# Layer norm with attention and a SwiGLU gate: the prologue's work is shared out anew among ScalarE, POOL and SP

## The chip, the cores and the metric

One core of one Trainium2 chip. The metric is the device time of one execution in microseconds; lower is better. The kernel before takes 1733.33 us (median of three runs, 1733.18 to 1734.9).

## The reference

```python
xn = layernorm(x)                       # x: 2048 tokens x 512, eps 1e-5
q, k, v = split(xn @ wqkv)              # 32 heads of 16
p = softmax(q @ k.T * 16**-0.5)         # full attention, 2048 x 2048 for each head
s = (p @ v) @ wo
h = silu(xn @ w1) * (xn @ w3)           # 1792 wide
return x + s * silu(h @ w2)
```

All in float32. A product of two float32 matrices is made of three matmuls on rounded parts: each operand is split into a high part (rounded) and a low part (the rest), and low x high, high x low and high x high are summed.

## The kernel before, in words

The 2048 tokens are 16 tiles of 128 (`t`) and four blocks of 512 (`b`).

**The prologue** (lines 449 to 668) normalises and transposes the tokens, makes the values of all heads, and the Q and K rows of the first eight heads. Its steps:
- `load_x(t)` fetches one token tile (nine buffers). Tiles 0 to 3 are fetched at the start; others as the work goes on.
- `spread(t)` makes mean and variance on VectorE (DVE), and the power -1/2 on POOL; `norm(t)` calls it, and normalises on DVE.
- `transposed(t)` turns a tile by four TensorE (PE) transposes; ScalarE (ACT) copies the high part, DVE makes the low part. Blocks 0 and 2 use one pair of buffers (`even_pair`), blocks 1 and 3 another.
- `token_rows(b, c)` multiplies a block with the K (`c` = 1) or Q (`c` = 0) weights: 12 matmuls; the high part by ACT, the low part by DVE; stored by ACT's and SP's queue. `load_k` and `load_q` fetch these rows back, arranged by head, in six copies each.
- `token_values(b, i)` multiplies one tile with the V weights: 12 matmuls, copies on ACT, a store from ACT's queue.
- `keep_tokens(b)` stores a block's transposed high and low part (1 MB each).
- `beside(b, n)` puts maxima of the first head pair between these steps, as many as `groups` says. One maximum (`max_unit`) is a matmul of 128 queries with 512 keys and a DVE reduction.
- `blank` lists arrays that POOL clears, among them `qs` and `ks[1]`, which `load_q` and `load_k` fill.

**The main stage.** There are 32 phases (16 head pairs, two halves of the queries). For each, the maxima of the scores are found first (`m`), they are appended to the queries as two more rows (`max_rows`, whose four copies to `qs` are line 446), and then come scores with their exponential on ACT (`s`) and the multiplication with the values (`v`). The gate's SwiGLU products (`f`) and the projection of the remaining Q and K rows (`rows_here`) run between them. Matmuls of `s`, `m` and `f` have at most 64 rows, so the upper and the lower half of the array work at the same time (small and capital letters). `ORDER_OF_ISSUE`, a text of some 9200 letters, says in which order the halves are issued; `r` and `R` place the row step, `o` the output's products. A letter whose work isn't ready by the kernel's own clock model is put off and issued later. PE takes its instructions in this order.

The gate's weights are fetched into four buffers, split by POOL and kept in a ring of nine places, the first four of which lie in `even_pair`; SP issues these loads in order with all its other copies. When the gate's last half is done, its memory is given back, and the loads for the output's products begin.

Seven PSUM banks are shared by all these products; the eighth (`pv`) holds the attention's sums.

Of the kernel before, what the change touches and what calls it, by code (L numbers as in the profile page):

```python
# [51 lines left out]
    "MfMfMffMMffMMffMffMffRfMffMfMffMmFfFFmFffFfFFfFFfFmFmFfffMffMffMfSFfFfsFFfFsfFFsmFFsFmFFffmFsFFmFsfF"  # L52
    "mFSfFsfMsFfFmSfFmFfSFfMfSffSsMvvvSmmFFsFsFffMsFFfmSfSfFmFsfFMsFFfmFMfSffMfSfmMvvMsSffMfFfSFmfSfFMsfF"
    "SmFfSfFmFsFFmsFFfmFMffMmMvvvSmsMFfFfFsfMFsfFmSfFsFmFsFfMsfFmFFfSfMffMfSMmvvSmSffMFfSfFmfSfFMsfFsFMff"
    "SFmSFfmFsFfFsFmMFfMmvvRsSMsFsvmSsFFmFfSfFfSmFfmSfFfSfFmFfSmFsFfMfFfMSfMmvvsMSsMmvFmsFFmFsFmFsFffSfMf"
    "SFfmSfFFmsFFffMMffMMsvvSfSsSmfMvvmSmSfFFfsFfMFsFfmSfFFsmFFsfMsFFfmFMfSffMfSfmMvvmSfSMfFfSfFmSffFMsFf"
    "FsMsFFfmsFFfMsFfmFFMfMfMmvvvMsfMSffSfFFmfSFmFsfFmFSfmFFsfFFmSffFFfMsfMMsvvRSmsFFmFsFffMfSFfFsmFsFfMs"
    "FfFmSfmFFfMffMsMvvsMfMfSfSfMfSffMsFfFmFsFFmfSfFsFmFfSFfSmfFfSmFFffMSffmFSfFmFfSmfFSfFsfFMsFfmFsFfFMf"
    "FsmFMmvvvsSFmmFMmvvvMsSffMfSfFFmfSFfMsFfSfMfSfFmFsFfMsFFfFffMSffMSfffMsFsFfFmFsFFmsFFfFmSfmFFsfMfFmM"
    "vvsMmSmSvvvsMmFFsfFFsfMsFfFmSfFsFmFSffMsfFmFFffSMffMfSMsvvRmSFsFfFmFsFfSmFsfFMffSfFMsfFFmSfmFFfSffMM"  # L60
    "mvvMfSfMfSffMfSfSffFMfSFfmSFffMsfFSfMfFsFmFsFmFsFFfmFfSfMMmvvmSmSmMvvMfSffMSfMffSfMfsFFsfFFmFsFfsMfF"
    "FsmFFsFfsMfFFmfSFfFssMfFfFmSfFsFmFFfMffSMfMfMfvvSssSsSvvvMssFFmsFmFFmFsFfFsfFFmSfFfSmFsfFMfSfFmfSFfM"
    "sFfSfMfSfFmFsFfMsFfMfSfMfFfSfMfMmvvMmMsMmvvvsMmFSfFfFsfMFsFfmSfFfSmFSfFfSmfFFsMfFsFfmFsFfMSfFfmFsFmF"
    "FsfFmFfMfSfSfSrvsSmSMmvvMffSMmmMvvFmFsFmsFmFFsFfFsfMsFfMfSfFsFmfFSfMsfFFmFsFmfFSffSFmFFsfMFfffMSfMff"
    "SfFFsmFFsFmFsfFmFSfFmSfmFfFFfMmmMvvvvSmfMfSFffSFmfSFmFsFmFfSfMFfsFfFsMSfFfmFFffMfSffMSfSffMFsFfmFsFm"
    "FsFFfmFsFFmfSfFFmmMvvsMmMMsvvmSSmMfrvmSfMfSSffFFmfSFmFsFmFfSfMfFsFfFsMSfFfmFFffMfSfMfSfSffMFsfFmFsFm"
# [12 lines left out]
    "fMfSffMSfMffSfFsFmFsFfFmSfFFmsFsFFfmFmFmMvvvMssSMmvfMSfMfSfMffSFfFsmFsFfMfSfmFFsFmFfSmfFFsmFFfMmvvvS"
    "mfMfSSfFfFmSfFfMsfFsFMsfFFmFsFfMsFfmFFMffSmMvvmSfFsMfFfSFmSffFSmFfSfMsFfFmSfFfMsFfFsFmFfSmSvvvvRMsMf"  # L80
    "fSFffSFfMsFffSMsFFfmSFffMsFMffFsFFmsFFffMsFFfmFsFfMsFfmFFsFFmfSfMFfsMFfFfMffMmMvvvMsfSfMfSfFFmFsFmFs"
    "fFFmSffFSmFfSfMfSfFmFfFfMfSfMfSfSffMfFsFmsFfFMsfFmFFsFFmsFFmfFmMvvvvMfSffMSffMfSfSfFmFsfFMsfFFmSFfFm"
    "sFfsFMFfsFmFffMSffMFfsFFmfSsFFfmFsFfMsFFfmSfFmfFFfmMMmvvvvmSSmfSfFfFFmfSfFSmFfSfFmfSFfmSfFFmFsFfFssM"
    "vvvvRfSMfSffMSffMFfsFmFfSsFFfmFsFfFmSfFFmsFfFfMMmvvMsfFsMFsFffMFsfMfSfMfFsFmfFSffFSmFsFfMsfFfMFffSMf"
    "SffSsSvvsSSsSsvvvMsSmmSvMffSMfSffMfSffSfMsFFfmSfFmFsFsFfFmFsFfMFsfFmFsFmFfSFsfFmFFsfFmSFffMfFMffMMfM"
    "fmMvvvvmSMsfFfFsFFmSfFmFsFfmFSfFmFsfFFsMfFsFmSFffMsFfmFSFfSfmSFffMSffFmSfMfMfMfFfsMvvvvRMsmFFssFFmFs"
    "FsFffFmFFsFmFsFFfmSffSFmSffFMfSfFmSfFMffSfMFfsMfFfSMfFfffMMfmMvvvvmSSfmFfFFsFmFsFmFsfFmFSfmFFssFFfMs"
    "fFFmsFFFmsfFmFFffSMfSMfffSfMfSfMfSfsFFfmFsFFmsFFfmFSfFmFsmFFfMffMmMvvvvSmSmFssFvvsMmFsFFfFsfMSffMfSf"
    "MfFsFmFfSfFfSmFfFfMfSfMfSffMsFsFFfFmFsFmsFfFFmSfFmFsfFfMfSfMmMvvMsSmmMvvmSMfFsfFFsfMsFFfmSfSfFmFsFfF"
    "mFfSfMfSfFmFfMmrvvSmSfFmsFfFfMsFFfmSfFsFmFFsFfmSFfmSfFffMfSfMMmvvvMsfSfMfSfFFmfSfFMsFfsFMfSfFmSffFMs"  # L90
    "FfsFFsFFffMfSffMFFfmFsFsfFMsFFfmFsFfMsFfFmFSfSfmMvvSsmSmMvvFmsFmFFsmFFsFffSfMSffMSffFMfsFMffSfSfFmFF"
    "ffMSffMfSfFmFsFFsfMFsFfmFsFFmsFFfmFMfMfmMvvvmSSmMmvvfMSffMSfMffSfFsFfMsFfFsFmFmFfSfsFFmSfFfFmFmrvMsf"
    "SMffFfSFmSfFfMsFfSmFfSfFmFsFFmsFFfmFMffMmSvvvvsMMffSFffSFmSfFmFsFmFfSfMfFsFSffMsFFfmfFFfMfSffMSffSfM"
    "sFfFmFsFmFsFFfmFsFFmsFfFMfMfSsSvvvvvmFsFmFFsFmFsFfSffMfSfMfSFfMfsFfMfSFfSfmFFffMSffMfsFFmFsFfFsMFfsF"
    "mFsFfMsFFfmFfMMffmMvvvmSSfMfFfsFfMfSfMfSfMfFsFmFfSfFsFmFsFfMsFfFmFfSfMfSffMsMvvmSSmSmvvvRfSMffSMffSf"
    "MfSfsFFmFFsfMfSfFmSfFFmfSffMFsSfFfMFsfFmsFFfMfSfFmsFmFFfSmfFFsFfFmMmvvvfMfSfMFsFfmFFsFmFsSffFMfFsfFS"
    "mFfsFMfsFFfMsFfFmSffFSfMsFfFmFsfFMfSffFMmfMvvvSmsMMmvvmFsFFmsFFmFsfFfSfMfSfMfSfFfMsFfMfSfSfFmSfFfMsF"
    "fFmFsFmFsFfFsFmSFfFfSfffMSsMvvvvvFmFsFmsFmFsFsFFmFmFsFffSfFMsfFmFSfFSfmSffFMSfFfmSFfmsFmFfFMmvvvMssM"
    "fFsFfFFfSmFfSmFfSfFmSfFfMfFsFmFsFfMfSfMrvmSmSsFFffFfMsFfFmSfFFsmFsFfMsFfmFSfFfMffSfMMmvvMsfSFmFfFsfM"
    "sFFfmSfFsFmFsFfMfSFfmSfFmFfSfMfSmvvvvFmsFmFFsFsFmFfSffMfSfMSfFffMsFfMfSfSfFmFFffMfSffMsFFmFsFFfsMFfs"  # L100
    "FmFsfFMsFfmFFMfffMMsvvsMSffMfSfFFmfSFfMsFfSmFSffFmFsFmFsFFfmFfSfMSmvvSmSsFmfFFffMFsfFmSfFsFmFsFfMsFf"
    "mFFffSMfMffSsMvvvvvRSmfSMffFSffFMsfFSfMfFsFmSffFMsFMffFsFFmsFFffMfSfFmFsFmFsFFfmFsFmFfSfMFfsFfMSfFff"
    "MmMvvsSSsmMvvvSmfMfSFfSfFmsFFmFsFmFfSfMFfsSfFfMSfFfmFfFfMfSfMfSffSfMsFfFmFsFmFsFFfmFsFFmFfFfMmMmvvMs"
    "MfmSMvvvMssFMsFfFfFmSfFfSmFfsFMfFsFfMsFfMfSffFFfMfSfMfSffMfSfsFFmFsfFMFsfFmSfFFmsfFfSFsFFsMmvvSmSssS"
    "vvvRSmFsfFFmFsFfmSfSfFmFsFfMsFfFmSfFmFfSfMffSfMSmvvvvSmsFmFfFFsfMFsFfmSfFSfmFfSFfmSFffMfSFffMFfMffSM"
    "ffSfFsFfMsfFFmFsFmFfSfmFFsmFFfFfMmmMvvvvMsfFfMsFFfMffSFmfSfFfSmFsFfFMsFfMfmFFfmFmMvvSmfSfMFfsFFmsFFf"
    "MsFfsFMfsFFfMsFfMfSffFFfMfSffMfSfMfSFfFsmsFFfMFsfFmsFFmFsFmFFfSffMmSvvvvSmfMfSfSfFFmfSfFMsFfsFMfFsfF"
    "MsfFMfSfsFFfmFFsSmvvvSmSfMfSffSfMmrvsMMffSfSfMfSffMfSfMfFsFmFfSfFFsmFFsfMfSfFmFsFmFsFfSfFmFFsfMSfFfm"
    "FsFFmsFfFfMSffMsSvvvvvFmFsmFsFFsmFsFmFFffSFmSFffMsfFfMSfSfFmfSfFMfSFfmSfFfMfSfMFfsFFmsFFffMMffMmMvvv"
    "SmSfMffSFfFmfSFfMsFfFsMfFsfFMsfFmFSfsFfFMfSfFmFsFfMfSffMFsFfsFMsfFFmFfFfMfSffMfMMfvvvvvRSmFsmFFfsFFf"  # L110
    "mFFsmFFsfFFmFsmFFsSffFMfsFFmFsFmFFffmFSffSFmFsfFMsfFmFSfFmfFSfFmSfmFFfsMfFmMvvvsMfSfMSffFFmfSFmFsFmF"
    "fSfMfFsSfFfMsFfFmFFffMfSfMfSfSffMsFFfmFsFmFsFfFmFsFmFFffFMmMmvvvmSmMMsvvfMfSMffSfMfSfFFsmFsfFMsfFmFF"
    "sFmfFSmFfSfFmFfsSvvvMsMsfFFfFsfMSffMfSFfMfsFmFfSfFsFmSFfFmFmFfMmvvmSMffSFfSfFmfSFmFsFmFfSfMFfsSfFfMf"
    "FsFmFFffMfSffMSffSfMsFfFmSfFFmsFFfmFsFFmsFfFFssMvvvvRfSfMSfMffSfMfFsFFmfSsFFfmFsFfFmSFfmFsFfFMfmSvvv"
    "vsMfMSffFfSFmSffFMsfFSmFfSFfmFsFmFsFfFmFMfMfsSvvvmFsFmFsFsFFmFffSfMfSfMfSFfMfsFfMfSffFSmFFffMfSfmFFs"
    "FmFsFsFfMfFsFmsFFfMsfFfMFfMffMmMvvvsMMfSfFfsFfMfSFfsMfFsFmFfSFmSfFfMsFFfmSfFFffMSffMfSfMffSFsFfmFFsF"
# [30 lines left out]
def raw(ap):  # L147
    return ap.bitcast(F32)
# [1336 lines left out]
```

## Time and profile before

| | |
|---|---|
| median of 3 runs | 1733.33 us |
| the profiled execution | 1733.92 us, span 1732.1 us |
| PE busy | 1704.7 us (98%) |
| DVE, ACT, POOL busy | 80%, 71%, 49% |
| DMA | 181.07 MB, 105 GB/s in the mean |
| mean granted clock of the core | 0.993 |

A busy share is an average over stages with different limits, and a busy PE need not be at its best pace: matmuls overlap, and a short wait between them is read as busy. So the first 150 us, the long middle and the end are looked at each by itself.

### The profile page before, as it was taken

The numbers are of one execution on the slowest core, as the hardware profiler recorded it, in microseconds if no ns is written. First come the engines' busy times: TensorE is split into PE (matmuls) and PEld (weight loads), VectorE is DVE, ScalarE is ACT, GpSimd is POOL, SyncE is SP. The second block draws the span as 40 slices with busy tenths as digits, with TensorE's granted clock in tenths as the row PEclk, the third lists the DMA queues.
The fourth block names the chain that finished last, engine by engine and source line by source line (L and its number), as shares of the span: only waits on it lengthen the run. The fifth ranks groups of instructions, "written<-read, shape, count | busy, mean of one in ns | idle before, by whom it ended". The sixth has DMA issues, their size and how long they took to land.

```text
span 1732.1 us, 35859 instructions
## 1 busy us (share of the span) xinstructions
PE 1704.7 (98%) x13476; PEld 1132.9 (65%) x13476; DVE 1389.7 (80%) x2313; ACT 1221.6 (71%) x2434; POOL 854.2 (49%) x887
## 2 busy tenths in 40 slices
PE   7989999999999999999999999999999999999998
PEld 5666666666766676666666666667667667665465
DVE  7787888888888787888888887878797868888735
ACT  3217777687768777777777777778777777878861
POOL 4026464266535664456556563556457716652201
PEclk8999999999999999999999999999999999999999
DMA  6674442242344452231435443241333222340732
GB/s 216 214 189 123 118 117 79 38 143 78 76 125 126 128 141 75 62 94 47 105 108 139 132 106 86 78 82 53 93 99 83 75 40 57 99 99 29 220 113 97
DMA packets 170892, 181.07 MB, mean 105 GB/s; under 512 B 43872, under 2 KB 115552, under 8 KB 167744
## 3 DMA queue, kind: packets, MB, share of 16 engines
q1 hardware_dynamic: 166400, 170.66, 36.2%
q10 hardware_dynamic: 4320, 8.13, 1.3%
q8 instruction: 106, 1.74, 0.4%
q14 instruction: 66, 0.54, 0.1%
HBM read 131.56 MB, written 46.11 MB: 103 GB/s over the span
## 4 chain that ended last, share of the span: by engine, by line
PE 89%; issue 5%; DVE 3%; DMA 1%; SPq 1%; ACT 0%; POOL 0%; ACTq 0%; POOLq 0%
PE f L992 31%; PE pv L698 25%; PE m L419 15%; PE e L682 14%; PE m L541 2%; DVE mp L421 1%; DVE xn L505 1%; DMA ks<-qk 0%; PE e L203 0%; PE e L201 0%; PE m L434 0%; DMA ovl<-o 0%; PE e L205 0%; PE m L514 0%; DMA wr<-in_A_wqkv_dram 0%
## 5 line engine op out<-in xcount | busy, mean ns | idle before, releaser
L421 DVE TENSOR_REDUCE mp<-m 128x1 f32<-128x512 f32 x2048 | 1277.1, 683 | 221.3 <-PE m L419 139.3
L685 ACT ACTIVATE pt<-e 128x512 f32<-128x512 f32 x2048 | 1061.6, 614 | 287.2 <-PE e L682 153.5
L419 PE MATMUL m<-ks,qs 62*128 62x512 f32 x2048 | 744.4, 413 | 3.8 <-DMA ks<-qk 2.1
L682 PE MATMUL e<-qs,ks 64*128 64x512 f32 x2048 | 740.4, 407 | 5.2 <-DMA qs<-ml 5.2
L698 PE MATMUL pv<-pt,vt 128*17 128x512 f32 x4096 | 479.1, 595 | 0.0
L419 PEld LDWEIGHTS m<-ks,qs 62*128 62x128 f32 x2048 | 349.0, 184 | 128.2 <-issue 39.8
L682 PEld LDWEIGHTS e<-qs,ks 64*128 64x128 f32 x2048 | 352.3, 185 | 101.5 <-issue 35.1
L698 PEld LDWEIGHTS pv<-pt,vt 128*17 128x17 f32 x4096 | 100.5, 97 | 250.2 <-issue 244.8
L992 PE MATMUL f<-xtl,wh 64*128 64x512 f32 x496 | 182.3, 391 | 0.0
L992 PE MATMUL f<-xth,wl 64*128 64x512 f32 x496 | 177.7, 393 | 0.0
L992 PE MATMUL f<-xth,wh 64*128 64x512 f32 x496 | 176.4, 392 | 0.0
L992 PE MATMUL f<-wh,hs 64*128 64x512 f32 x528 | 165.9, 392 | 0.0
L992 PE MATMUL f<-xtl,xeh 64*128 64x512 f32 x448 | 164.4, 393 | 0.0
L992 PE MATMUL f<-xth,xeh 64*128 64x512 f32 x448 | 161.8, 394 | 0.0
L992 PE MATMUL f<-xth,xel 64*128 64x512 f32 x448 | 160.3, 395 | 0.3 <-DVE mp L421 0.3
L842 POOL TENSOR_TENSOR h<-g,h 128x512 f32<-128x512 f32 x56 | 72.0, 1286 | 176.4 <-ACT h L838 172.6
L340 POOL TENSOR_TENSOR wl<-wr,wh 128x512 fp32r<-128x512 f32 x105 | 135.2, 1288 | 8.8
L992 PE MATMUL f<-xeh,hs 64*128 64x512 f32 x368 | 118.8, 394 | 0.0
L340 POOL TENSOR_TENSOR xel<-wr,xeh 128x512 fp32r<-128x512 f32 x87 | 112.1, 1288 | 7.3
L339 POOL TENSOR_SCALAR xeh<-wr 128x512 fp32r<-128x512 f32 x87 | 53.9, 619 | 105.0 <-PE f L992 33.8
L992 PE MATMUL f<-wl,hs 64*128 64x512 f32 x264 | 97.7, 392 | 0.0
L339 POOL TENSOR_SCALAR wh<-wr 128x512 fp32r<-128x512 f32 x105 | 64.9, 618 | 63.6 <-PE f L992 45.8
(212 smaller groups left out, 2147.4 us busy)
## 6 DMA issues: line engine op xcount, KB each, us to landing
wr<-in_B_w_dram SPq DMA_DIRECT2D x168, 256.0 KB
qs<-qk SPq DMA_DIRECT2D x186, 64.0 KB
ks<-qk SPq DMA_DIRECT2D x90, 128.0 KB
ovh<-xt SPq DMA_DIRECT2D x36, 256.0 KB
ovl<-xt SPq DMA_DIRECT2D x36, 256.0 KB
wr<-in_A_wqkv_dram SPq DMA_DIRECT2D x30, 256.0 KB
qk<-ch SPq DMA_DIRECT2D x24, 256.0 KB
qk<-c SPq DMA_DIRECT2D x24, 256.0 KB
```

What stands on the lines that cost most here:

```text
L339: nc.gpsimd.tensor_scalar(hi, t, 1.0, 1.0, op0=ALU.mult, op1=ALU.mult)
L340: nc.gpsimd.tensor_sub(lo, t, raw(hi))
L419: nc.tensor.matmul(ps, qs[p % 2][64 * h:64 * h + KM, q0:q0 + P], ks[p % 2][64 * h:64 * h + KM, c * 512:(c + 1) * 512], start=True, stop=True)
L421: nc.vector.reduce_max(mp[p, half][:, h, qt, c:c + 1], ps, axis=AX.X)
L505: nc.vector.tensor_scalar(xn, xin[t], mv[:, 0:1], rs, op0=ALU.subtract, op1=ALU.mult)
L541: nc.tensor.matmul(ps, lhs, wv[k][h == 1], start=n == 0, stop=n == len(three) - 1)
L682: nc.tensor.matmul(ps, ks[p % 2][64 * h:64 * h + KR, k * P:(k + 1) * P], qs[p % 2][64 * h:64 * h + KR, q0:q0 + 512], start=True, stop=True)
L685: done = nc.scalar.activation(pt, ps, AF.Exp, scale=DH ** -0.5)
L698: nc.tensor.matmul(pv[32 * j:32 * j + VW, :], vt[2 * p // GH][:, key, 2 * p % GH + j % 2, :], pt, start=key < 2 if last else k == 0, stop= ...
L842: nc.gpsimd.tensor_mul(h2, g, h2)
L992: nc.tensor.matmul(ps, left[r], right[r], start=starts and lane == 0, stop=ends and lane == 1)
```

## The change

Before the attention:
- All 16 token tiles have a buffer. Tiles 2 to 7 are fetched right after the first four weights, tiles 8 to 15 two by two during the values of block 0.
- `spread` runs ahead: tiles 3 to 7 during block 0's values, then each four tiles ahead of its use. For tiles 4 to 15 POOL also makes `nb` = -mean x rs, and ACT normalises (`Identity` with scale and bias). Tiles 0 to 3 stay on DVE.
- `token_rows` of blocks 0 to 2: ACT copies the product as it is, and POOL makes high and low part. Block 3 stays as it was. The stores are now `keep_rows`, from SP's queue alone, at moments of their own.
- The stores of tokens and rows and the loads `load_k`, `load_q` stand at other places. The arrays are cleared one at a time, the two `qs` during block 0's values.
- Block 2 uses the pair `rows2`, so that `even_pair` is free after block 0.
- `groups`: in block 3 the four maxima of step 2 move to steps 3 and 4, which have eight each.

Later:
- `load_k(1)` and `load_v(1)`, which stood at the prologue's end, are issued ahead of the gate's products 4 and 10; the gate's fetch of tokens begins with product 2.
- Row projections in the first half of a gate pass stand before products 0, 3, 6 and at the end instead of 0, 2, 5 and the end.
- `ORDER_OF_ISSUE` is another text.

```diff
-        return {0: (0, 2, 5, FH), 1: ()}[hf] if n < KC - 1 else ()
+        return {0: (0, 3, 6, FH), 1: ()}[hf] if n < KC - 1 else ()
...
-        load_x(2)
-        load_x(3)
+        for t in range(2, NT // 2):
+            load_x(t)
...
+            if t >= TB:
+                nb = pro.tile([P, 1], F32, tag="nb", name="nb", bufs=6)
+                nc.gpsimd.tensor_scalar(nb, mv[:, 0:1], rs, -1.0, op0=ALU.mult, op1=ALU.mult)
+            of[t] = mv, rs, nb
...
+            if nb is None:
+                nc.vector.tensor_scalar(xn[t], xin[t], mv[:, 0:1], rs, op0=ALU.subtract, op1=ALU.mult)
+            else:
+                nc.scalar.activation(xn[t], xin[t], AF.Identity, bias=nb, scale=rs)
...
-                xts[b] = xt_pair(keep) if b % 2 else even_pair()
+                xts[b] = xt_pair(keep) if b % 2 else rows2 if b else even_pair()
...
         for t in range(4):
-            of = spread(t + 2)
+            for n in ((2,), (3, 4), (5, 6), (7,))[t]:
+                spread(n)
...
-            load_x(t + 4)
-            xn[t + 2] = norm(t + 2, *of)
+            norm(t + 2)
             if t < 2:
                 split_w(KC + t, nc.gpsimd)
+            for n in range(2):
+                load_x(8 + 2 * t + n)
+            if t > 1:
+                nc.gpsimd.memset(*next(blank))
...
-        groups = {(1, 1): 4, (1, 2): 4, (1, 4): 4, (1, 5): 4, (3, 2): 4, (3, 3): 6, (3, 4): 6}
+        groups = {(1, 1): 4, (1, 2): 4, (1, 4): 4, (1, 5): 4, (3, 3): 8, (3, 4): 8}
...
-            nc.scalar.copy(sh, ps)
-            nc.vector.tensor_sub(sl, ps, raw(sh))
-            cols = slice(b * 512, (b + 1) * 512)
-            nc.scalar.dma_start(raw(qk_d[rbk][0])[:, cols], raw(sh))
-            nc.sync.dma_start(raw(qk_d[rbk][1])[:, cols], raw(sl))
+            if b == TB - 1:
+                nc.scalar.copy(sh, ps)
+                nc.vector.tensor_sub(sl, ps, raw(sh))
+            else:
+                sc = pros.tile([P, 512], F32, tag="sc", name="sc", bufs=2)
+                nc.scalar.copy(sc, ps)
+                nc.gpsimd.tensor_scalar(sh, sc, 1.0, 1.0, op0=ALU.mult, op1=ALU.mult)
+                nc.gpsimd.tensor_sub(sl, sc, raw(sh))
+            made_rows[b, c] = sh, sl
...
         for b in range(TB):
-            if b == 0:
-                keep_tokens(b)
             token_rows(b, 1)
-            if b == TB - 1:
+            if last:
+                keep_rows(b, 1)
                 load_k(0, cols)
...
             token_rows(b, 0)
-            if b < TB - 1:
-                load_k(0, cols)
+            if last:
+                keep_rows(b, 0)
+                load_q(0, 1)
             else:
-                load_q(0, 1)
-                load_k(1)
+                keep_rows(b, 1)
+            if b == 0:
+                keep_tokens(b)
             beside(b, 1)
             more_tokens(4 * b + (5 if b else 6))
             if b == 0:
                 more_tokens(7)
+            r = next(blank, None)
+            if r:
+                nc.gpsimd.memset(*r)
+            if b == 0:
+                keep_rows(b, 0)
+                load_k(0, cols)
                 load_q(0, 0, cols)
                 continue
             for i in range(TB):
                 run(token_values(b, i))
...
+                if not last:
+                    if i == 0:
+                        keep_rows(b, 0)
+                        load_k(0, cols)
+                    if i == 1 and b < TB // 2:
+                        load_q(0, 0, cols)
+                    if i == 1 and b == TB // 2:
+                        load_q(1, 0)
+                    if i == 2:
+                        keep_tokens(b)
+                    if i == 3 and b == TB - 2:
+                        wts.start()
+                elif i == 0:
                     wts.pump(KC)
                     wts.fill()
...
-        load_v(1)
...
-                    some_tokens()
+                    if number == 4:
+                        load_k(1)
+                        keys[1] = mod.now + 9.0
+                    elif number == 10:
+                        load_v(1)
+                    if number > 1:
+                        some_tokens()
```

More of the change, by code (lines that the diff above doesn't have):

```diff
@@ L57 @@
[L57 to L66, printed above, removed]
@@ L451 @@
         wqk = [[pro.tile([P, KC, P], F32R, name=f"w{c}{v}") for v in "hl"] for c in "qk"]
-        xin = [pro.tile([P, D], F32, tag="xin", name=f"xin{t}", bufs=9) for t in range(4)]
+        xin = [pro.tile([P, D], F32, tag="xin", name=f"xin{t}", bufs=NT) for t in range(4)]
         def load_x(t):
             if t >= 4:
-                xin.append(pro.tile([P, D], F32, tag="xin", name=f"xin{t}", bufs=9))
+                xin.append(pro.tile([P, D], F32, tag="xin", name=f"xin{t}", bufs=NT))
             nc.sync.dma_start(xin[t], x[t * P:(t + 1) * P, :])
@@ L486 @@
         busy(22)
-        xts = {}
+        xts, of, xn = {}, {}, {}
         def spread(t):
@@ L550 @@
         nc.gpsimd.memset(raw(ks[0]), 1.0)
-        xn = {0: norm(0)}
+        blank = iter([(raw(t), 0.0) for t in qs] + [(r, 1.0) for r in (raw(ks[1]), rb)])
+        spread(0)
+        norm(0)
         split_w(0)
         split_w(1, nc.gpsimd)
-        of = spread(1)
+        spread(1)
         transposed(0, xn.pop(0))
         busy(6)
-        xn[1] = norm(1, *of)
+        norm(1)
         split_w(2, nc.gpsimd)
@@ L868, in counted @@
                             fetch_tokens(rest[0])
-                    some_tokens()
+                    if number == 4:
[3 more added lines that the diff above has]
+                        load_v(1)
+                    if number > 1:
+                        some_tokens()
                 for f in range(FH):
@@ L1238 @@
     count = {"S": 0, "M": 64, "V": 0, "chunks": 0, "phase": 1}
-    keys = {0: 0.0, 1: 0.0}
+    keys = {0: 0.0}
     rooms = []
-    rows, outs = [[2.0, first_rows, 2, 0]], []
+    rows, outs = [[3.0, first_rows, 2, 0]], []
     stored = {}
```

215 lines of the change are left out of this document (106 added, 109 removed).

## The prediction

> **What bounds the kernel now.** I read the first part of the page, then busy time by stage, then what TensorE (PE) waited for.
>
> ```profile
> PE 1704.7 (98%) x13476; PEld 1132.9 (65%) x13476; DVE 1389.7 (80%) x2313; ACT 1221.6 (71%) x2434; POOL 854.2 (49%) x887
> ```
> ```profile
> 0.00:150.00 150.00, 128.68 (x641) 92.89 (x641) 110.55 (x196) 46.09 (x94) 48.14 (x62) 0.93 0.67 209
> 140.00:1500.00 1360.00, 1359.18 (x11335) 913.01 (x11332) 1129.03 (x1873) 1033.27 (x2056) 748.87 (x768) 1.00 0.36 93
> 1600.00:1733.00 133.00, 126.82 (x767) 71.77 (x764) 71.69 (x115) 75.20 (x153) 18.55 (x18) 0.99 0.43 140
> ```
>
> The columns of the second fence are: stretch, length, busy time and instructions of PE, weight load, VectorE (DVE), ScalarE (ACT) and POOL, granted TensorE clock, DMA share, GB/s. From 140 to 1500 us PE is busy 1359 of 1360 us at clock 1.00; no other engine is near full. So a saved microsecond of another engine is worth nothing there, and time can only be won where PE is idle, slow or badly fed: 150 - 128.7 = 21.3 us idle in the first 150, and the end, where PE carries fewer instructions per microsecond. What is lost in the first 150 us has two parts, low clock and waits:
>
> ```profile
> 30.00:35.00 5.00, 2.20 (x8) 1.43 (x8) 4.20 (x9) 0.93 (x2) 0.84 (x2) 0.50 0.03 11
> 35.00:40.00 5.00, 0.79 (x1) 0.29 (x1) 4.20 (x4) 0.24 (x1) 4.04 (x3) 0.50 0.63 193
> 40.00:45.00 5.00, 4.24 (x14) 3.40 (x15) 2.19 (x6) 0.06 (x1) 0.55 (x1) 0.63 0.12 29
> 50.00:55.00 5.00, 5.00 (x18) 3.90 (x19) 4.20 (x10) 0.59 (x1) 0.55 (x1) 0.66 0.65 197
> ```
> ```profile
> PE e L682 <- DMA qs<-ml: 5.2, 1, 5.2
> PE m L514 <- DVE xn L505: 4.7, 2, 3.0
> PE e L203 <- DVE xtl L518: 4.7, 1, 4.7
> PE m L419 <- DMA ks<-qk: 2.1, 2, 1.2
> PE m L419 <- issue: 1.3, 1, 1.3
> ```
>
> Busy time times the missing clock is 1.1 + 0.4 + 1.6 + 1.7 = 4.8 us on top of the idle 21.3. Of the idle time, 5.2 us are the start of the attention, 9.4 the normalised tokens of the second block and their low parts. The rest is small or at the very start.
>
> **The step from block 0 to block 1.** These are PE, DVE and POOL rows in order of time (start, length); the first is the last product of block 0's Q projection, the second the second product of block 1's K projection.
>
> ```profile
> 27.29 0.39 PE L205 MATMUL e<-xeh,wqh 128*128 128x512 f32 x1
> 40.77 0.80 PE L203 MATMUL e<-xtl,wkh 128*128 128x512 f32 x1 [4.68 <-DVE xtl L518]
> 36.38 3.74 DVE L505 TENSOR_SCALAR xn<-xin,mv,rs 128x512 f32<-128x512 f32 x1 [0.73 <-POOL rs L498]
> 36.29 1.80 POOL L647 MEMSET qs<- 128x2048 f32 x1
> 38.03 1.80 POOL L648 MEMSET qs<- 128x2048 f32 x1
> ```
> ```profile
> L505 DVE TENSOR_SCALAR xn<-xin,mv,rs 128x512 f32<-128x512 f32 x16 | 16.8, 1047 | 8.8 <-POOL rs L498 8.8
> L517 ACT CAST xth<-m 128x512 fp32r<-128x512 f32 x8 | 4.6, 587 | 9.7 <-PE m L514 9.7
> L518 DVE TENSOR_TENSOR xtl<-m,xth 128x512 fp32r<-128x512 f32 x8 | 5.4, 679 | 0.3 <-ACT xth L517 0.3
> L339 POOL TENSOR_SCALAR wh<-wr 128x512 fp32r<-128x512 f32 x4 | 2.5, 617 | 5.1 <-PE f L992 5.1
> ```
>
> From 27.7 to 40.8 is 13.1 us in which PE does only two groups of four transposes. The chain is serial on DVE: load, statistics, POOL's power, normalise, transpose, split, for each token, with nothing run ahead. The normalisation that takes 3.74 us starts with a POOL clearing and ends 3.8 us later with a second one, so it stood still under both; the mean of the 16 is 1.05.
>
> The change takes 12 of these 16 normalisations to ACT, runs the statistics two to four tokens ahead, has every token loaded before block 1, and moves the four clearings (two pairs here) one by one to later places. What is left between the Q projection's end and the second product of block 1 is ACT's queue and one low part: the copy of Q's rows 0.59, high part 0.59, normalisation of a later token about 0.6 (an ACT pass over 128x512 like the high part), high part 0.59, low part on DVE 0.68, five handovers of about 0.1: 3.6 us, and 0.4 for statistics that stand between the low parts. I take 4.0 of 13.1: **9.1 us gained**. Bounds: 3 (if POOL's power and the new negative bias, behind low parts on POOL, are late for each token) and 11. The gap still ends in a slow spell like that of 40 to 45, so I count no clock here.
>
> A sentence on the clock: the wait by "issue" of 1.3 us just ahead of 50 was enough for the slow stretch 50 to 55. The Trainium skill (TensorE: Matmul & The Clock Gate, "What's actually happening") has the half clock only after an idle window of about 3.4 us; the trace disagrees, with 0.66 granted after 1.3 us idle. By that rule the 1.7 us of the stretch would be gained too, and the sum would be 1.7 larger; I go by the row.
>
> **The start.** Loads 2 to 7 now stand in SP's queue before the K and Q weights, four more than before (x4 to x7).
>
> ```profile
> 11.15 0.62 ACT L524 CAST wkh<-wr 128x512 fp32r<-128x512 f32 x1
> 10.00:15.00 5.00, 4.97 (x26) 3.75 (x26) 4.14 (x9) 2.62 (x6) 3.49 (x7) 1.00 0.97 305
> ```
>
> 4 x 262 KB at 305 GB/s is 3.4 us. The cast of the K weights at 11.15 waited for nothing, so its data had slack; ACT now may stand there for 0 to 3.4 us, and with it the high part of the third token and PE. I take **1.5 us lost**, nearer the lower end, since PE has products of the first token to do meanwhile.
>
> **K and Q rows of blocks 0 to 2.** The high part moves from ACT to POOL and the low part from DVE to POOL, and both stores are issued by SP (before, the high one by ACT), K's and Q's at fixed later moments. DVE loses 6 low parts, POOL gains 6 pairs.
>
> ```profile
> L340 POOL TENSOR_TENSOR wl<-wr,wh 128x512 fp32r<-128x512 f32 x4 | 5.1, 1267 | 0.3
> L498 POOL TENSOR_TENSOR rs<-ve,minus 128x1 f32<-128x1 f32 x16 | 8.8, 550 | 56.0 <-DVE ve L496 55.9
> 99.98 2.19 DMA qk<-sh
> 102.54 2.05 DMA ks<-qk
> 34.50 2.69 SPq L398 DMA_DIRECT2D ks<-qk  x6
> 49.88 0.70 PE L419 MATMUL m<-ks,qs 62*128 62x512 f32 x3 [1.35 <-issue]
> ```
>
> After the Q projection of block 0: copy 0.59, up to two small POOL operations of 0.55 ahead in the queue, high part 0.62, low part 1.27, together about 3.6 with handovers; then the store 2.2, six K copies and six Q copies at 0.45 each, of which the first six hide the store (2.7), then 2.7, then 2.05 to land: 3.6 + 2.7 + 2.7 + 2.05 = 11 us. PE in that time: 4.0 (above) + K projection partly at half clock 3.6 (12 of the 14 instructions of the row from 40 to 45) + transposes 0.5 + Q projection 2.8 (12 products; from 10 to 15 a PE instruction took 0.19, shorter transposes among them) = 10.9. So the first maxima (at 49.88 before, after 1.35 us of waiting) wait about as now: **0**, with -7 as one end (a rival below) and +3 (wait and slow spell gone) as the other. All queued behind this wait is PE itself, since its queue is in order.
>
> **Blocks 2 and 3.** DVE has here no statistics, normalisations or low parts of rows left.
>
> ```profile
> 73.89 0.73 PE L419 MATMUL m<-ks,qs 62*128 62x512 f32 x4
> 77.91 1.60 PE L419 MATMUL m<-ks,qs 62*128 62x512 f32 x4
> 117.45 5.47 DVE L421 TENSOR_REDUCE mp<-m 128x1 f32<-128x512 f32 x9 [0.36 <-PE f L992]
> ```
>
> Four maxima take 0.73 us where banks are free and 1.60 where DVE is behind with its reductions; block 2 has one more such group. I gain 2 x 0.87 = **1.7 us**. In block 3 the four maxima after the first value product are taken out, and the two later groups grow from 6 to 8. That removes the wait for K rows (2.1 us in two waits), and costs bank waits: 8 reductions of 0.61 (nine in 5.47 us in the last row) against seven banks, about 0.9 a group. **+0.2**.
>
> **The start of the attention.** SP's queue in order:
>
> ```profile
> 121.11 0.38 SPq L390 DMA_DIRECT2D vt<-v  x1
> 128.82 0.80 SPq L446 DMA_DIRECT2D qs<-mh  x1
> 131.06 0.64 SPq L446 DMA_DIRECT2D qs<-ml  x1
> ```
>
> The load of the second value group waits for the last value store and leaves at 121.11; the gate's weights stand behind it, and one of these holds the four row copies (L446) until 128.82. PE waits 5.2 us. The change takes this load and that of the second keys out of this place (to products 10 and 4 of the gate) and lets token copies begin two products later. 12 maxima instead of 9 go ahead of the row step, so its DVE part comes 3 x 0.61 = 1.8 us later, and there are 55 instead of 44 gate halves before the first score. From the first gate product: DVE 0.9 + 12 x 0.61 + 0.2 = 8.4 us, four copies 2.9, landing 1.3: scores at 12.6; 21 maxima at DVE's pace keep PE until about 11. The wait is about 1.0 to 1.6 instead of 5.2, and a short slow spell behind it goes too: **4.2 us gained** (0 to 5.7). Late next: nothing on SP; the second keys' load has some 20 us between its product and the first maximum that reads it.
>
> **The main stage.** The issue order is written anew, row projections stand at 3 and 6 instead of 2 and 5. The letters are the same in number (4608 halves of the gate, 2048 scores, 1984 maxima, 512 value steps), in 206 runs of value steps instead of 204, and after 1000, 2000 ... 8000 letters the gate's halves differ by 12 at most. **0**, with 5 either way.
>
> **The end.** 136 score and 40 maximum letters followed the last gate half; now 65 scores and no maximum do.
>
> ```profile
> 1560.00:1570.00 10.00, 10.00 (x88) 8.05 (x88) 9.35 (x16) 9.15 (x18) 3.64 (x5) 1.00 0.20 55
> 1630.00:1640.00 10.00, 10.00 (x70) 4.31 (x67) 5.74 (x10) 9.71 (x20) 0.00 (x0) 1.00 1.00 358
> ```
>
> In the second row ACT is busy 9.7 of 10 and PE holds 70 instructions instead of 88: scores at ACT's pace, without gate work between them, about 2 us lost in ten. I take some 30 us to be like it, about 6 lost, since 71 scores more and 40 maxima fill this stretch now. About half of those scores now run beside the gate: **3 us gained** (0 to 7).
>
> Sum: 9.1 - 1.5 + 0 + 1.7 + 0.2 + 4.2 + 0 + 3 = 16.7 us. The profiled execution took 1733.92 (span 1732.1), 0.6 above the median; from the median 1733.3 I get **1717**.
>
> **Rivals.**
> First, the transfers take the place of the waits. The two 1 MB token stores of block 0 now leave shortly ahead of Q's rows and the loads of K and Q. 2.1 MB at 305 GB/s are 6.9 us; if the loads land that much later, the first maxima wait 7 us more, and the sum is 9.7: 1724. For it: all go through SP. Against: the DMA share was 0.03 to 0.65 in the four slow stretches from 30 to 55 us, so there is room. The Trainium skill (DMA: Bandwidth & Descriptors, "Queues, rings and completion order") says that descriptors of one issuer's ring are taken in ring order; by that the whole 6.9 us would be paid. No row here separates it.
>
> Second, slower: the new order feeds PE worse. The matmuls' weight loads already wait for banks that DVE and ACT have not freed:
>
> ```profile
> PEld m L419 <- DVE mp L421: 29.0, 52, 1.5
> PEld e L682 <- DVE mp L421: 24.0, 33, 0.9
> ```
>
> These are 53 us, nearly all inside a stage that reads as fully busy. If the new mix enlarges them by two fifths, 21 us are lost: 1733.3 - 16.7 + 21 = 1738. It decides from about a third on. Against: the counts by thousand letters are nearly equal.
>
> Third, no change: PE saves time at first, but the loads of the end, which may start only after the last gate half, now begin later against the remaining work, and PE waits there for about as long as was won: 1733. For it: fewer letters stand after that half, for the same loads. Against: these are 8 MB by the code, 26 us at 305 GB/s, and most of the output's products still stand behind them.
>
> Fourth, more: the first maxima wait for nothing and the slow spells go: 16.7 + 3 + 3.3 = 23: 1710.
>
> **How the numbers follow.** Forecast 0.53, transfers 0.22, slower 0.10, no change 0.07, more 0.08. A change of 0.2% (3.5 us) is about what can be told here. Faster is 0.53 + 0.22 + 0.08 = 0.83, same 0.07, slower 0.10. The range 1705 to 1731 takes in forecast, transfers and most of "more", and leaves out the two that hold 0.17.
>
> **What would show it.** Right: PE's idle sum in the first 150 us near 10 instead of 21.3, block 1's K projection at about 33, the first maxima near 42, scores starting 14 us before 133; no wait of SP for value stores near the gate's start; weight loads waiting for DVE about as long as now; fewer than 10 us from the last gate half with ACT above 9.5 of 10. Wrong: a wait of the first maxima above 3 us; ACT standing for weights near 12; instructions in 140 to 1500 below 8.2 per us; PE waiting for transfers after the last gate half.

## The result and the profile after

The changed kernel took 1715.06 us (median of 4 runs, 1714.13 to 1717.6) beside 1734.12 us of the kernel before on the same chip: a ratio of 0.9892, interval 0.9874 to 0.9909, 19 us less. The forecast was 1717. The profiled execution took 1717.6, the slowest of the four.

The first part of the page of the changed kernel, and its busy time by stage (columns as in the prediction):

```profile
PE 1700.4 (99%) x13476; PEld 1125.9 (66%) x13476; DVE 1376.2 (80%) x2295; ACT 1228.0 (72%) x2446; POOL 868.4 (51%) x911
```
```profile
0.00:150.00 150.00, 140.71 (x781) 100.91 (x784) 112.61 (x208) 64.98 (x127) 73.29 (x98) 0.98 0.65 209
40.00:45.00 5.00, 3.42 (x11) 2.32 (x12) 2.64 (x5) 0.68 (x2) 1.12 (x1) 0.60 0.73 245
45.00:50.00 5.00, 5.00 (x20) 3.58 (x19) 2.34 (x6) 1.42 (x3) 1.27 (x3) 0.71 0.21 52
140.00:1500.00 1360.00, 1360.00 (x11344) 908.64 (x11338) 1128.00 (x1871) 1032.03 (x2061) 745.60 (x764) 1.00 0.36 93
1610.00:1620.00 10.00, 10.00 (x67) 4.26 (x63) 5.85 (x11) 9.68 (x20) 0.00 (x0) 1.00 0.24 73
```

PE's idle time in the first 150 us fell from 21.3 to 9.3 us, its low clock there from 5.7 to 2.8 us (busy time times missing clock; before, 130 to 140 adds 0.9 to the 4.8 of the prediction). Together that is 14.9 of the 16.3 us between the two spans. From 140 to 1500 us PE does 11344 instructions instead of 11335.

A shorter reading says the same, and serves for every kernel below: count PE's instructions in the first 150 us. Of 13476, 781 are done by then instead of 641. The rest takes (13476 - 641) / (1732.1 - 150) = 8.11 instructions per us before and (13476 - 781) / (1715.8 - 150) = 8.11 after; 140 instructions at that rate are 17.3 us. In all fourteen kernels of this study the rate after 150 us lies between 8.107 and 8.116, which is 0.9 us either way over the rest. So whatever the change won, it won before 150 us.

What PE waited for most in the changed kernel:

```profile
PE m L419 <- DMA qs<-qk: 3.2, 2, 1.8
PE e L201 <- ACT xth L522: 1.5, 1, 1.5
PE m L419 <- ACT vt L553: 1.3, 3, 0.7
PE m L546 <- ACT xeh L522: 0.8, 1, 0.8
PE e L203 <- DVE xtl L523: 0.7, 1, 0.7
```

Before, the scores' row copies (5.2), the normalised tokens (4.7) and their low parts (4.7) led this list. The first two are gone, the low parts are 0.7, a wait for high parts (`xth`) is 1.5, and a new one leads: 3.2 us of the first maxima for Q's rows.

The PE rows of the changed kernel that answer to the prediction's: the last product of block 0's Q projection, the first two of block 1's K projection, the first maxima, the third and fourth group of maxima of block 2 (1.60 and 1.63 us before), the first gate product and the first score.

```profile
28.42 0.40 PE L205 MATMUL e<-xeh,wqh 128*128 128x512 f32 x1
31.17 0.50 PE L201 MATMUL e<-xth,wkl 128*128 128x512 f32 x1 [1.48 <-ACT xth L522]
32.39 0.50 PE L203 MATMUL e<-xtl,wkh 128*128 128x512 f32 x1 [0.72 <-DVE xtl L523]
...
40.15 0.47 PE L419 MATMUL m<-ks,qs 62*128 62x512 f32 x1 [1.76 <-DMA qs<-qk]
42.05 1.19 PE L419 MATMUL m<-ks,qs 62*128 62x512 f32 x3 [1.43 <-DMA qs<-qk]
...
71.14 0.73 PE L419 MATMUL m<-ks,qs 62*128 62x512 f32 x4
75.15 0.73 PE L419 MATMUL m<-ks,qs 62*128 62x512 f32 x4
...
106.00 0.50 PE L1023 MATMUL f<-xth,xel 64*128 64x512 f32 x1
118.39 0.39 PE L706 MATMUL e<-qs,ks 64*128 64x512 f32 x1
```

The gap between the blocks is 28.82 to 32.39, 3.6 us, where it was 13.1. The scores start at 118.39 without a wait, 14.6 us earlier; from the first gate product it is 12.4 us, where it was 16.0.

### The profile page after: what moved, and what is told of

It reads as the page before. It is cut to its first block, busy times and chain, and to the rows that moved or that the text cites. A ratio compares the mean times of both kernels' runs of the same rounds, so it can differ in the third digit from the quotient of the medians.

```text
span 1715.8 us, 35891 instructions
## 1 busy us (share of the span) xinstructions
PE 1700.4 (99%) x13476; PEld 1125.9 (66%) x13476; DVE 1376.2 (80%) x2295; ACT 1228.0 (72%) x2446; POOL 868.4 (51%) x911
## 4 chain that ended last, share of the span: by engine, by line
PE 92%; issue 2%; DVE 2%; DMA 2%; SPq 1%; POOL 1%; ACT 0%; ACTq 0%; DVEq 0%; POOLq 0%
PE f L1023 32%; PE pv L722 26%; PE m L419 16%; PE e L706 15%; PE m L546 2%; DVE mp L421 1%; DMA wr<-in_A_wqkv_dram 1%; SPq L758 0%; DMA ovh<-o 0%; PE m L434 0%; DMA inh<-in_A_x_dram 0%; PE e L201 0%; PE m L519 0%; PE o L201 0%; PE e L205 0%
## 5 line engine op out<-in xcount | busy, mean ns | idle before, releaser
L1023 PE MATMUL f<-xtl,xeh 64*128 64x512 f32 x440 | 160.4, 391 | 0.0
L1023 PEld LDWEIGHTS f<-wh,hs 64*128 64x128 f32 x528 | 92.3, 185 | 4.8 <-POOL hs L868 1.0
```

The lines of the kernel that those rows point to most:

```text
L1023: nc.tensor.matmul(ps, left[r], right[r], start=starts and lane == 0, stop=ends and lane == 1)
```

## The experiments

All were timed in five rounds against the kernel before. That kernel's own median lay between 1733.3 and 1736.2 us in the different series, so kernels are compared by their ratios to it.

**1. Is it the prologue or the order of issue?** The changed kernel with the old order of issue:

```diff
 ORDER_OF_ISSUE = ( ...the old one... )
-        return {0: (0, 3, 6, FH), 1: ()}[hf] if n < KC - 1 else ()
+        return {0: (0, 2, 5, FH), 1: ()}[hf] if n < KC - 1 else ()
-    rows, outs = [[3.0, first_rows, 2, 0]], []
+    rows, outs = [[2.0, first_rows, 2, 0]], []
```

> The changed kernel with the old issue order, the old places of the row projections (0, 2, 5, end) and the old start of the row step; everything ahead of the attention, and the late loads of the second keys and values, stay as changed. Theory A (the gain was made ahead of the first scores, the new order is worth at most 2 us): 1715 to 1719, scores starting between 118 and 121 us. Rival B (the new order, with the gate's halves drawn out to the end, brings 5 us or more): 1720 or more, with the excess after 1500 us.

1716.16 us, ratio 0.9889 (0.9875 to 0.9902), against 0.9892 of the whole change. The new order and the shorter tail behind the last gate half bring nothing that shows in the time. The scores start at 115.44, earlier than the 118 to 121 expected.

**2. The reverse**: the kernel before with the new order, its places and its start, and nothing else of the change.

> The kernel before with only the new issue order, the new places of the row projections and the new start of the row step; its prologue and the loads of the second keys and values at its end stay. Theory A: 1730 to 1735, PE idle in the first 150 us 18 to 21 (the wait for the rows shrinks a little, since 55 gate halves stand ahead of the first score instead of 44). Rival B: 1728 or less, the gain after 1500 us.

1737.99 us, 1.0016 (1.0007 to 1.0026): slightly slower, where no loss was expected. PE did 617 instructions by 150 us instead of 641, 24 fewer (3 us), and went on at the same rate; the tail gained none. Its idle time by 150 us was as before (21.5 against 21.3); what was lost is clock around the attention's start: from 120 to 145 us, busy time times missing clock was 4.1 us instead of 0.9.

**3. The loads of the second keys and values put back** to the prologue's end, the token copies back to the gate's first products:

```diff
+                load_k(1)          # with the last block's beside(b, 1)
...
+        load_v(1)                  # at the end of the prologue
...
-                    if number == 4:
-                        load_k(1)
-                    elif number == 10:
-                        load_v(1)
-                    if number > 1:
-                        some_tokens()
+                    some_tokens()
```

> The changed kernel with the loads of the second keys and values back at the prologue's end, and the gate's fetch of tokens from product 0 again. Theory A: SP stands at the value load until the last value store has landed (near 110 us), weights and row copies come later, PE waits 2 to 5 us for the rows ahead of the first score: 1717 to 1720. Rival: the row step is late enough by its 12 maxima on DVE, the load is hidden: within 1 us of the changed kernel.

1725.82 us, 0.9951 (0.9939 to 0.9964): 10 us of the 19 are gone, more than expected. SP's queue of this kernel, in order of time, then the waits of SP and PE that matter here and one row of its stages:

```profile
110.14 0.38 SPq L390 DMA_DIRECT2D vt<-v  x1
...
121.58 0.38 SPq L325 DMA_DIRECT2D wr<-in_B_w_dram  x1
122.06 0.80 SPq L446 DMA_DIRECT2D qs<-mh  x1
```
```profile
SPq L390 <- DMA v<-vrow: 5.7, 1, 5.7
PE e L708 <- DMA qs<-ml: 9.3, 1, 9.3
```
```profile
120.00:130.00 10.00, 4.48 (x25) 3.99 (x26) 1.92 (x3) 2.61 (x5) 8.63 (x10) 0.55 0.75 216
```

The same two kinds of rows in the changed kernel, where the row copies leave at 113.87:

```profile
113.45 0.37 SPq L325 DMA_DIRECT2D wr<-in_B_w_dram  x1
113.87 0.80 SPq L446 DMA_DIRECT2D qs<-mh  x1
```

An issue that has to wait holds everything behind it in SP's queue. SP stands 5.7 us at the value load, for the last value store. The gate's weights leave behind it and the row copies behind these, 8.2 us later than in the changed kernel, though their data was ready at 111.5. The token copies, which this run moves back too, also go out in between; but the last three weight loads (117.72, 119.65 and 121.58) each leave as POOL ends a split, so it is the weights that set the pace. PE stands 9.3 us and then runs at 0.55 of its clock.

The wait is longer than the 5.2 us of the kernel before. Two parts of the way to the row copies have grown. From the first gate product to the value load it is 6.9 us instead of 4.2: that product came 13.6 us earlier than before (103.28 against 116.92), the value load only 11.0 (110.14 against 121.11). From the value load to the row copies it is 11.9 instead of 7.7, and 11.8 in experiment 2 too, so this part goes with the new order. Neither the order alone (experiment 2, 4.7 us) nor an earlier prologue alone lengthens PE's wait: in experiment 9 the first gate product comes 7.2 us earlier, the value load 7.4, and the wait is 5.2 us as before.

**4. Block 0's token store behind K's and Q's loads** (the changed kernel otherwise):

```diff
-            if b == 0:
-                keep_tokens(b)
...
                 load_q(0, 0, cols)
+                keep_tokens(b)
                 continue
```

> The changed kernel with block 0's token store (2 x 1 MB) moved behind the loads of K and Q that the first maxima wait for. If SP's transfers land in the order of issue, these loads had up to 6 us of the store ahead of them: the waits of 1.8 and 1.4 us ahead of the first maxima fall to below 1 in sum and the slow stretch from 40 to 50 us goes, 1710 to 1713. If the loads overtake the store or share with it, the waits stay above 2.5 and the time is within 1 us.

1714.5 us, 0.9879 (0.9865 to 0.9892). First SP's rows of the changed kernel, then SP's and PE's of this one:

```profile
28.34 0.39 SPq L632 DMA_DIRECT2D xt<-xeh  x1
33.14 4.05 SPq L398 DMA_DIRECT2D ks<-qk  x6
37.24 2.73 SPq L407 DMA_DIRECT2D qs<-qk  x6
```
```profile
33.01 2.86 SPq L398 DMA_DIRECT2D ks<-qk  x6
35.91 2.73 SPq L407 DMA_DIRECT2D qs<-qk  x6
38.74 0.37 SPq L632 DMA_DIRECT2D xt<-xeh  x1
...
39.73 1.08 PE L419 MATMUL m<-ks,qs 62*128 62x512 f32 x4
```

Without the two stores ahead of them, six K copies take SP 2.86 instead of 4.05 us and the first maxima wait for nothing. Not all of that is the stores' doing. In this run block 1's K projection ran at a lower clock, as this row shows (in the changed kernel such a product takes 0.40), so PE came to the maxima at 39.80 instead of 38.39:

```profile
32.71 0.63 PE L205 MATMUL e<-xth,wkh 128*128 128x512 f32 x1
```

And in experiments 1 and 3, where the stores stand as in the changed kernel and the six K copies take 4.03 and 4.04 us, the K projection was slow as well, and the first maxima waited 1.0 and 0.9 us instead of 3.2. So the delay of 1.2 us at the issue is real; how much of the 3.2 us it makes is not shown. PE's count by 150 us rises from 781 to 806, but experiments 5 and 7 reach 796 and 798 with the stores in place. In the times the intervals of the two kernels overlap, and 1714.5 lies above the 1710 to 1713 expected.

By the Trainium skill (DMA: Bandwidth & Descriptors, "Queues, rings and completion order"), descriptors of one ring are consumed in ring order. The prediction had all 6.9 us of the two stores paid by that rule. But the stores leave at 28.34 and 28.82, the first K copy at 33.14, and the DMA engines are full from 29 to 36 us (a share of 0.89 or more). So only some 3 us of stores were left ahead of the copies, an estimate from these times; what was measured does not speak against the rule.

**5. All normalisations on DVE**, the statistics still ahead; no token gets a bias, so `norm` takes DVE's branch for all:

```diff
-            if t >= TB:
+            if t >= NT:
                 nb = pro.tile([P, 1], F32, tag="nb", name="nb", bufs=6)
```

> The changed kernel with all 16 normalisations on DVE (no negative bias on POOL); statistics still run ahead. Theory A1 (the gap between block 0 and block 1 closed mainly because the statistics run ahead and POOL's clearings are out of the way): the gap of 1.5 + 0.7 us ahead of block 1's K projection grows by 1 to 3, 1716 to 1719. Theory A2 (it closed because DVE no longer normalises): the gap grows by 5 or more, 1721 or more.

1715.55 us, 0.9891 (0.9878 to 0.9905): the same as with ScalarE. The gap between the blocks is 4.9 us (28.78 to 33.66) instead of 3.6, as theory A1 said, but the first maxima then wait for nothing, so that it does not show in the time.

**6. Statistics no longer ahead**, ScalarE still normalises, from token 6 on:

```diff
         def norm(t):
+            if t >= 6:
+                spread(t)
             mv, rs, nb = of.pop(t)
...
-            for n in ((2,), (3, 4), (5, 6), (7,))[t]:
+            for n in ((2,), (3, 4), (5,), ())[t]:
...
-                if n + 4 < NT:
-                    spread(n + 4)
```

> The changed kernel with the statistics of tokens 6 to 15 made right before their normalisation, as the kernel before did; ACT still normalises. Theory A1: each normalisation now waits for 1.0 us of DVE, 0.8 of POOL and the handovers, the gap ahead of block 1's K projection grows by 3 to 6 us: 1719 to 1723. Theory A2: ACT's own queue is what counts, less than 2 us: 1714 to 1717.

1728.23 us, 0.9965 (0.9952 to 0.9977): 12.6 us of the 19 are gone, above the range of either theory. The gap between the blocks is 11.0 us (28.69 to 39.72). What PE waited for in it, and two of ScalarE's rows:

```profile
PE m L521 <- ACT xn L513: 4.6, 2, 3.5
PE e L201 <- ACT xth L524: 4.0, 1, 4.0
```
```profile
33.06 0.81 ACT L513 ACTIVATE xn<-xin,nb,rs 128x512 f32<-128x512 f32 x1 [2.83 <-POOL nb L502]
...
37.66 0.81 ACT L513 ACTIVATE xn<-xin,nb,rs 128x512 f32<-128x512 f32 x1 [2.83 <-POOL nb L502]
```

Each token costs ACT a wait of 2.8 us for POOL's bias, 4.6 us from one normalisation to the next. Experiments 5 and 6 together: the changed kernel needs the statistics ahead, and in its time it is of no account which engine normalises. Neither run puts the clearings back in pairs; experiments 9 and 11 have them so.

**7. High and low parts of K's and Q's rows by ScalarE and DVE in all blocks**, in `token_rows`; the stores stay on SP:

```diff
-            if b == TB - 1:
+            if b >= 0:
                 nc.scalar.copy(sh, ps)
                 nc.vector.tensor_sub(sl, ps, raw(sh))
```

> The changed kernel with the high and low parts of the Q and K rows made by ACT and DVE in all four blocks, as before; stores and loads stay where the change has them. POOL's 12 operations (11.4 us) go, DVE gets 6 of 0.69 back. By my sum POOL's part is worth 1.7 us through DVE's shorter queue in block 2: 1716 to 1718. Rival: POOL's detour of about 3 us delays the rows that the first maxima wait for, so that without it these maxima come 1 to 3 us sooner: 1712 to 1714.

1713.69 us, 0.9883 (0.987 to 0.9897): POOL's low parts are not needed. The time lies in the rival's range. K's copies leave at 31.59 instead of 33.14 and the first maxima wait for nothing, as the rival has it; but the K projection ran slowly in this run too, and the intervals overlap, so a gain is not shown.

**8. Tokens 4 to 7 fetched behind the K and Q weights:**

```diff
-        for t in range(2, NT // 2):
+        for t in range(2, 4):
             load_x(t)
...
+        for t in range(4, NT // 2):
+            load_x(t)
```

> The changed kernel with tokens 4 to 7 fetched behind the K and Q weights instead of ahead of them. ACT's wait of 1.6 us for the K weights and PE's of 0.8 behind it go; the time falls by 0.5 to 1.5 us (1713.5 to 1714.5). Rival: the statistics of tokens 3 and 4 then wait for their data and the wait only moves: within 0.4 us of the changed kernel.

1715.72 us, 0.9893 (0.9878 to 0.9907): nothing to be had at the start. ACT's wait for the K weights is gone and PE's wait of 0.8 us for `xeh` in the list above fell to 0.5, but ACT stands 2.3 us later on, behind POOL's split of the Q weights. That the wait only moves was the rival.

**9 to 11. The two pieces alone, built into the kernel before.** First, tokens fetched early and statistics ahead only; second, late loads only; third, both. All three keep the old order, the old stores, DVE's normalisations and low parts.

```diff
 statistics ahead, against the kernel before
-        load_x(2)
-        load_x(3)
+        for t in range(2, NT // 2):
+            load_x(t)
...
-            of = spread(t + 2)
+            for n in ((2,), (3, 4), (5, 6), (7,))[t]:
+                spread(n)
...
 loads late, against the kernel before
-                load_k(1)
...
-        load_v(1)
...
-                    some_tokens()
+                    if number == 4:
+                        load_k(1)
+                        keys[1] = mod.now + 9.0
+                    elif number == 10:
+                        load_v(1)
+                    if number > 1:
+                        some_tokens()
```

> The kernel before with one thing of the change: all tokens fetched first and the statistics run ahead as in the change; normalisation and low parts stay on DVE, ACT still issues the high rows' stores, clearings in pairs, old order, old loads at the prologue's end. Theory C (two pieces make the gain, the statistics ahead and the late loads of the second keys and values): the gap ahead of block 1 closes by about 8 us, but the value load then stops SP ahead of the row copies as in the run with the loads put back, 1722 to 1727. Rival D (ACT's and POOL's new work is needed as well, since the clearings still hold the normalisations on DVE): 1728 or more.

> The kernel before with only the loads of the second keys and values moved to the gate's products 4 and 10 and the gate's fetch of tokens from product 2 on. Theory C: the wait of 5.2 us for the rows falls below 2 and its slow stretch goes, 1727 to 1730. Rival: without the earlier prologue the row step itself (DVE) is what ends late, 1731 or more.

> The kernel before with both pieces, statistics ahead and late loads, and nothing else of the change (old order, DVE normalises and makes the low parts). Theory C: nearly the whole gain, 1714 to 1719. Rival D: 1721 or more.

| kernel | us | ratio | interval | PE instructions by 150 us |
|---|---|---|---|---|
| statistics ahead | 1727.21 | 0.9951 | 0.9937 to 0.9964 | 692 |
| loads late | 1727.59 | 0.9951 | 0.9939 to 0.9964 | 677 |
| both | 1719.44 | 0.9905 | 0.9892 to 0.9919 | 750 |
| whole change | 1715.06 | 0.9892 | 0.9874 to 0.9909 | 781 |

PE's waits with statistics ahead alone, then with late loads alone:

```profile
PE e L683 <- DMA qs<-ml: 5.2, 1, 5.2
PE m L512 <- DVE xn L504: 3.5, 2, 3.0
PE e L203 <- DVE xtl L516: 1.7, 1, 1.7
```
```profile
PE m L514 <- DVE xn L505: 4.9, 2, 3.0
PE e L203 <- DVE xtl L518: 4.7, 1, 4.7
```

Each piece takes away its own wait and leaves the other's, and by the ratios they add up (0.49% and 0.49%, together 0.95%). In this series the kernel before took 1736.2 us; with the ratios taken from 1733.3 the three come to 1724.8, 1724.8 and 1716.9, so the first and the third lie where theory C had them and late loads gain more than it said. They are worth 8.5 us alone, 8.0 where statistics run ahead and 10.2 in experiment 3, too close for these intervals to tell apart.

Statistics ahead alone do not close the gap between the blocks as far as expected, 5.4 us instead of 8: it is still 7.7 (28.89 to 36.54). The clearings, in pairs as before, hold DVE's normalisation there, which takes 0.54 us where nothing disturbs it:

```profile
29.56 2.67 DVE L504 TENSOR_SCALAR xn<-xin,mv,rs 128x512 f32<-128x512 f32 x1
30.15 1.81 POOL L637 MEMSET ks<- 128x2048 f32 x1
36.54 0.79 PE L203 MATMUL e<-xtl,wkh 128*128 128x512 f32 x1 [1.67 <-DVE xtl L516]
```

With both pieces the gap is 7.7 us as well; in experiment 5, where DVE normalises too but the clearings stand apart, it is 4.9. So clearing one at a time counts in the gap; no run has it alone.

The same kernel shows where block 2's gain comes from: with statistics ahead alone its maxima are all as fast as in this row, with late loads alone two groups still take 1.63 and 1.60 us.

```profile
75.39 0.74 PE L419 MATMUL m<-ks,qs 62*128 62x512 f32 x4
```

Both pieces together give 16.5 of the 19 us; the rest of the change is worth some 2 us, within the intervals.

**12. The best of these together**: the changed kernel with experiments 4 and 7.

> The changed kernel with block 0's token store behind the loads of K and Q, and the rows' high and low parts made by ACT and DVE in all blocks. The two gave 0.9879 and 0.9883 alone against 0.9892 of the changed kernel; if they remove the same wait, 1713 to 1715, if they add, 1711 to 1713.

1712.36 us, 0.9867 (0.9853 to 0.988), the fastest of all and in the range for gains that add, though its interval overlaps that of the change as it stands. Its stages:

```profile
30.00:40.00 10.00, 7.58 (x37) 5.61 (x37) 6.31 (x15) 4.31 (x8) 5.01 (x9) 1.00 0.59 198
40.00:50.00 10.00, 10.00 (x50) 7.58 (x48) 9.39 (x19) 5.40 (x10) 2.10 (x5) 1.00 0.76 282
0.00:150.00 150.00, 141.92 (x819) 101.23 (x821) 118.64 (x219) 69.96 (x138) 65.27 (x88) 1.00 0.65 209
```

PE is idle 8.1 us in the first 150, none of them is followed by a low clock, and 819 instructions are done.

## Why the prediction was right, and where it was not

The time (1717 for 1715) and the sign came out as said, and so did PE's idle time (near 10; 9.3). Of the terms of the sum some were right and others cancelled. Two of the signs that the prediction had named for being wrong came as well: the first maxima waited for more than 3 us (3.2), and ACT stood for the K weights near 12 us (1.6 us, until 13.16).

- **Block 0 to 1, 9.1 us.** Right in size: 4.0 us were to be left, 3.6 are. The working put ScalarE's normalisation and the moved clearings beside the statistics. Experiments 5, 6 and 9 separate them in part: statistics ahead are needed and close 5.4 us of the gap by themselves, the clearings that still stand in pairs hold part of the rest, and ScalarE's share is some 1.3 us in the gap and nothing in the time. The price of about 0.6 us for a normalisation on ACT was too low: the rows above show 0.81. Its handovers of 0.1 each come from no row; the last one took 0.06 (a low part ends at 32.33, PE starts at 32.39).
- **Start, -1.5 us.** Mis-sized. PE waits 0.8 us there, and experiment 8, which undoes the cause, gains nothing measurable.
- **First maxima, 0.** Wrong in part. From the end of Q's projection (28.8) the chain was to take 11 us; the first maximum starts after 11.3 (40.15), the other three after 13.2 (42.05). And PE arrived after 9.6 us instead of 10.9, because its K projection ran at full clock. So it waits 3.2 us and then runs at 0.60 and 0.71. That is the place of the rival "the transfers take the place of the waits", with 3.2 us instead of 7. The stores have a part in it (experiment 4); but the wait was 1.0 and 0.9 us in experiments 1 and 3, with the same stores and a slow K projection, so its size is also a matter of the clock.
- **Blocks 2 and 3, 1.7 and 0.2 us.** The two slow groups of block 2 take 0.73 us, as said. That POOL took over the low parts is not why: with them on ScalarE and DVE the groups are as fast (experiment 7), and statistics ahead alone bring it (experiment 9). In block 3 the wait for K rows (2.1 us) is gone, and 0.6 us of waits for `vt` on ACT have come there, 0.7 more right behind it.
- **Start of the attention, 4.2 us (0 to 5.7).** The mechanism and the time from the first gate product to the scores were right (12.6; 12.4). The size was not: the wait of 5.2 us is gone whole, and by the times 8 to 10 us hang on these loads (experiments 3 and 9 to 11). What makes the rest beside the wait is shown only in experiment 3, where the new order and the changed prologue would have made it 9.3 us, with a slow spell behind it.
- **The main stage, 0.** Right: from 140 to 1500 us nothing changed. The order's letters for value steps are 500 and 503, in 203 and 206 runs, not 512 in 204 and 206; nothing hangs on that.
- **The end, 3 us.** Not there. As the prediction's sign had it, behind the last gate half (1631.43) ACT is no longer above 9.5 of 10 in any ten. But the stretch at ACT's pace has only moved ahead of that half: from 1610 to 1620 above it is 9.68 of 10, with 67 PE instructions, and experiments 1 and 2 show no gain from order or tail. That such a stretch costs 2 us in ten was not shown to matter.
- **The order.** The rival "slower" had weight loads waiting longer for DVE. They wait less:

```profile
PEld m L419 <- DVE mp L421: 23.4, 43, 0.9
PEld e L706 <- DVE mp L421: 19.7, 32, 0.9
```

  These are 43 us instead of 53, and it makes no difference to the rate after 150 us.
- **The clock.** The prediction counted a slow spell of 1.7 us after a wait of 1.3 us, against the Trainium skill (TensorE: Matmul & The Clock Gate, "What's actually happening"), by which only an idle window of some 3.4 us brings one. The changed kernel's slow spell does not decide it: the waits of 1.76 and 1.43 us before it have one matmul of 0.47 us between them, 3.66 us in all. Experiment 4 agrees with the row: at block 1's K projection PE was never idle for more than 1.48 us, and the clock from 30 to 35 us was 0.74.

So the total was right partly by luck: the attention's start brought some 4 to 6 us more than its term, the end's 3 us did not come, and the first maxima waited about 2 us longer than before instead of as long. What is left unsettled is how the last 2 us divide among ScalarE's normalisation, POOL's clearings and SP's stores: the traces show the clearings and the stores at work, but each is below what these intervals tell apart.

## What to carry to other kernels

Before pricing the move of work to an idle engine, look for what in an in-order chain can be computed ahead: here two to four tokens of statistics were worth 8 us in the old kernel and 12 in the new one, and the engine that normalises nothing in the time. Where stages meet, read the issuing queue in order of time: one load that waits for a store holds every copy behind it, and its price must be taken from the kernel as it will be, with its own order: the same load cost 5.2 us of waiting in the old kernel and would have cost 9.3 in the new one. And count the bottleneck engine's instructions up to a fixed moment: it shows in one number in which stage the time was won. A wait of one profiled execution is not yet a cause: the first maxima waited 0.9 to 3.2 us with the same stores ahead of them, by how fast PE had come there.

## What the runs showed of the hardware

- The clock fell after short waits, but not after each: 1.76 and 1.43 us were followed by 0.60, while 1.48 and 0.72 us at 31 to 32 us in the same run left it at 1.00. Nor is it the length of the wait or the work before it: in experiments 1, 3 and 4 the same two waits at the same place (1.48 and 0.71 us) were followed by products of 0.63 instead of 0.40 us. What decides it no run here shows.
- ScalarE's normalisation, with scale and bias given per row, took 0.82 us for 128x512, its copy of the same size 0.59.
- A DVE normalisation took 0.54 us alone, 2.67 us beside POOL's clearings (experiment 9, above), and 1.19 us beside a POOL subtraction of the same size. These are rows of experiment 5:

```profile
33.52 0.54 DVE L509 TENSOR_SCALAR xn<-xin,mv,rs 128x512 f32<-128x512 f32 x1
40.60 1.19 DVE L509 TENSOR_SCALAR xn<-xin,mv,rs 128x512 f32<-128x512 f32 x1
```
```profile
40.22 1.29 POOL L621 TENSOR_TENSOR sl<-sc,sh 128x512 fp32r<-128x512 f32 x1
```

  The slow one began 0.4 us after POOL's operation and ended 0.3 us after it, as if it had been held until that was nearly done.
